# Moving the wait for the output's store from SyncE to GpSimd, which gathers the closing barrier

## The chip, the cores and the metric

One core of a Trainium2 chip. The metric is the device time of one execution in microseconds (us).

The argument plays in the last 2.5 us of a program of 1270 us, so much of it is told in ns. Those numbers are read from the raw records of the traces (start and duration of each instruction, and the time of each semaphore update, to the ns); the views of the profile round starts to 0.1 or 0.01 us. "Landing" is the last increment of the output's semaphore, that is the moment at which the stored output is known to be in memory. "+214" means 214 ns behind the landing of the same trace.

## The reference

Decode attention over a long cache, mixed with a small MLP. Only its shape matters here: 547 MB are read and 1,792 bytes are written.

```python
# K and V cache: [2, 8, 32768, 256] bfloat16 each; x: [2, 1, 448]
def reference(A_x, A_k_cache, A_v_cache, A_wq, A_wo, B_x, B_w1, B_b1, B_w2, B_b2, gate_w):
    x = A_x
    g = _sigmoid((x * gate_w).sum(-1, keepdims=True))
    a = _A_ref(x, A_k_cache, A_v_cache, A_wq, A_wo)      # attention of one query row
    b = _B_ref(x, B_w1, B_b1, B_w2, B_b2)                # gelu MLP
    return g * a + (1 - g) * b                           # [2, 1, 448] bfloat16
```

## The kernel before

Each engine has a program of its own; semaphores order them. GpSimd only prepares constants in the first 5 us. SyncE issues all big loads and, last, the store of the output, for which it waits. The block that holds the five programs ends in a barrier that the language adds: every engine executes a DRAIN, which here ends only after the engine's own last work; the other four then each add one to a gather semaphore, and GpSimd waits for four and releases them.

```python
        def prog_pool(E):
            E.ins(lambda e: e.memset(ident_b[:], 0.0), key="ms0")
            # ... constants, all done after 5.3 us
            for b in range(Bn):
                E.ins(lambda e, b=b: e.affine_select(...), key=f"ts{b}")

        def prog_sp(E):
            # ... every load of weights, K and V
            E.wait_total("mix")                     # both halves of the output are computed
            dma(lambda e: e.dma_start(out[:, 0, :], out_sb), "d_out", "out")
            E.wait_total("d_out")                   # the wait that is moved

        # ... prog_pe, prog_act, prog_dve
        with nc.Block("main") as block:
            def run(nm, eng):
                engs[nm].eng = eng
                progs[nm](engs[nm])

            block.gpsimd(lambda eng: run("pool", eng))
            block.sync(lambda eng: run("sp", eng))
            block.tensor(lambda eng: run("pe", eng))
            block.scalar(lambda eng: run("act", eng))
            block.vector(lambda eng: run("dve", eng))
```

## Time and profile before

| | |
|---|---|
| time, median of 6 runs | 1271.62 us (1271.50 to 1271.81) |
| span of the profiled run | 1269.955 us (shown as 1270.0), its time 1271.76 |
| store issued / landed / last instruction ends | 1268.403 / 1269.558 / 1269.955 us |

The prediction below shows the lines on which the reading rests. One more view helps to calibrate: the program opens with the same barrier as it ends with. These are rows of it (source line 889 of the kernel before: engine, operation, count, then the duration in ns as least/median/most, then the first and last start in us):

```profile
L889 POOLq EVENT_SEMAPHORE  x2: 17/17/17, 0.6 to 0.7; - x2
...
L889 POOLq DRAIN  x1: 187/187/187, 0.3 to 0.3; - x1
...
L889 SPq DRAIN  x1: 121/121/121, 0.5 to 0.5; - x1
```

GpSimd's gather and its release are again 17 ns long and start 79 ns apart (0.607 and 0.686 in the raw records). The recorded duration of such an instruction is a fifth of the step that it costs.

### The profile page before, as it was taken

To read this page: it belongs to the slowest core of one execution; us is meant where nothing else is said; L and a number is where in the kernel's file an instruction comes from. 1 tells how busy PE (TensorE), PEld (TensorE's weight loads), DVE (VectorE), ACT (ScalarE), POOL (GpSimd) and SP (SyncE) were. 2 spreads that over 40 slices of the span, in tenths; PEclk is the share of its full clock that TensorE was granted. 3 is DMA by queue.
4 is the path that set the end of the run, shared out by engine and by line. 5 is a ranking of instruction groups with operands and counts; after the bars stand their busy time and mean duration, and the time that the engine had idled before them with its cause. 6 is when DMAs were issued, how large, how long until landed. Compare 5 with 4: busy or idle time off the path is not lost.

```text
span 1270.0 us, 7459 instructions
## 1 busy us (share of the span) xinstructions
PE 698.5 (55%) x4386; PEld 140.6 (11%) x1842; DVE 689.9 (54%) x311; ACT 44.8 (4%) x184; POOL 4.4 (0%) x19
## 2 busy tenths in 40 slices
PE   0976456644466454565545666444764446655455
PEld 0211011100011110111001111000110001111012
DVE  4575536655365563556735466453665636557351
ACT  0100000000000000000000000000000000000000
POOL 1000000000000000000000000000000000000000
PEclk9877788777788777877768887678877778877787
DMA  9999999999999999999999999999999999999998
GB/s 408 450 429 430 430 431 436 442 431 430 429 431 438 431 438 438 431 431 429 431 438 431 436 440 431 429 431 431 440 429 436 440 431 429 431 431 440 429 425 369
DMA packets 11114, 547.58 MB, mean 431 GB/s; under 512 B 1368, under 2 KB 1632, under 8 KB 2144
## 3 DMA queue, kind: packets, MB, share of 16 engines
q1 hardware_dynamic: 10948, 547.43, 99.7%
q8 instruction: 7, 0.11, 0.0%
q10 hardware_dynamic: 156, 0.01, 0.0%
q14 instruction: 3, 0.02, 0.0%
HBM read 547.43 MB, written 0.00 MB: 431 GB/s over the span
## 4 chain that ended last, share of the span: by engine, by line
DMA 58%; PE 20%; DVE 15%; issue 5%; another core or an unknown queue 2%; ACT 0%; ACTq 0%; SPq 0%; DVEq 0%
DMA ring<-in_A_k_cache_dram 54%; DVE ring L760 12%; PE ps_s L527 7%; PE ps_s L342 6%; PE ps_o L342 4%; DMA ring<-in_A_v_cache_dram 3%; PE ps_o L576 1%; DMA PT<-in_gate_w_dram 1%; DVE mx L764 1%; PE ps_m L541 0%; PE ps_m L536 0%; PE ps_f L588 0%; DVE gmax L766 0%; PE ps_o L470 0%
## 5 line engine op out<-in xcount | busy, mean ns | idle before, releaser
L760 DVE STREAM_TRANSPOSE ring<-ring 128x4096 uint32<-128x4096 uint32 x128 | 557.6, 4413 | 385.0 <-DMA ring<-in_A_k_cache_dram 384.7
L527 PE MATMUL ps_s<-ring,Abd 128*128 128x512 bf16 x1024 | 427.9, 418 | 399.7 <-DVE ring L760 399.2
L342 PE MATMUL ps_s<-ring,Abd 128*128 128x512 bf16 x1024 | 424.4, 414 | 0.0
L527 PEld LDWEIGHTS ps_s<-ring,Abd 128*128 128x128 bf16 x1024 | 106.2, 104 | 822.1 <-DVE ring L760 456.6
L342 PE MATMUL ps_o<-ring,PT 128*24 128x512 bf16 x1504 | 112.0, 405 | 0.0
L546 PE MATMUL ps_f<-o_sb,selg 128*32 128x257 f32 x32 | 17.0, 635 | 91.1 <-DVE o_sb L793 89.9
L576 PE MATMUL ps_o<-ring,PT 128*24 128x512 bf16 x544 | 56.6, 415 | 14.3 <-DMA ring<-in_A_v_cache_dram 14.3
L764 DVE TENSOR_REDUCE mx<-ps_s 128x1 f32<-128x1024 f32 x16 | 19.6, 1225 | 60.8 <-PE ps_s L342 60.8
L677 ACT ACTIVATE negm<-ps_m 128x1 f32<-128x1 f32 x16 | 2.7, 171 | 1133.7 <-PE ps_m L541 1133.7
L777 DVE STREAM_TRANSPOSE PT<-pexp 128x1024 bf16<-128x1024 bf16 x16 | 19.9, 1245 | 36.7 <-PE ps_o L342 36.7
L793 DVE TENSOR_REDUCE o_sb<-ps_o 128x256 f32<-128x2048 f32 x15 | 34.4, 2291 | 0.5
L791 DVE TENSOR_TENSOR ps_o<-ps_o,mask 128x2048 f32<-128x2048 f32 x15 | 34.3, 2290 | 0.0
L576 PEld LDWEIGHTS ps_o<-ring,PT 128*24 128x24 bf16 x544 | 14.5, 98 | 103.9 <-issue 85.2
L774 DVE COPY ls<-lsum 128x1 f32<-128x1 f32 x16 | 2.5, 154 | 32.0 <-ACT pexp L681 32.0
L671 ACT COPY Abd<-qrep 32x16 bf16 (+1 forms) x128 | 19.5, 199 | 0.6
L681 ACT ACTIVATE pexp<-ps_s,negm 128x1024 bf16<-128x1024 f32 x16 | 17.8, 1114 | 1.7
L536 PE MATMUL ps_m<-ident_f,mx 128*1 128x128 f32 x32 | 6.1, 271 | 21.1 <-DVE mx L764 21.1
L441 PE MATMUL ps_o<-ring,xT 128*32 128x512 bf16 x16 | 5.0, 501 | 20.4 <-issue 20.4
L546 PEld LDWEIGHTS ps_f<-o_sb,selg 128*32 128x32 f32 x32 | 2.9, 140 | 109.2 <-DVE o_sb L793 107.1
L541 PE MATMUL ps_m<-ones_f,gmx 1*128 1x1 f32 x32 | 6.3, 262 | 9.9 <-DVE gmx L770 9.9
L807 DVE TENSOR_SCALAR o_sb<-ps_o,mask 128x256 f32<-128x256 f32 x1 | 0.5, 484 | 17.0 <-PE ps_o L342 17.0
L766 DVE TENSOR_REDUCE gmax<-ps_m 1x2 f32<-1x128 f32 x16 | 4.5, 278 | 7.5 <-PE ps_m L536 7.5
(87 smaller groups left out, 75.3 us busy)
## 6 DMA issues: line engine op xcount, KB each, us to landing
ring<-in_A_v_cache_dram SPq DMA_DIRECT2D x1, 4096.0 KB, 27.2
ring<-in_A_v_cache_dram SPq DMA_DIRECT2D x2, 2048.0 KB, 34.0
ring<-in_A_wq_dram SPq DMA_DIRECT2D x1, 3072.0 KB, 28.5
ring<-in_B_w_dram SPq DMA_DIRECT2D x1, 1568.0 KB, 34.5
ring<-in_A_wo_dram SPq DMA_DIRECT2D x1, 1568.0 KB, 37.9
ring<-in_B_w_dram SPq DMA_DIRECT2D x1, 1344.0 KB, 32.2
ring<-in_A_wo_dram SPq DMA_DIRECT2D x1, 1008.0 KB, 39.8
ring<-in_A_wo_dram SPq DMA_DIRECT2D x1, 560.0 KB, 40.7
```

The source lines that it names most:

```text
L342: return e.add_instruction(mybir.InstMatmult(name=f"I-{nc.next_id()}", engine=mybir.EngineType.PE, ldweights=False, ins=[e.lower_ap(x), e. ...
L527: fn = lambda e, o=o, x=x, st=st, sp=sp, s=s, w=w: e.matmul(o, a_win(s, w), x, start=st, stop=sp, skip_group_check=True)
L541: E.ins(lambda e: e.matmul(ps_m[:, C_BC:C_BC + 1], gmx[:, :], ones_f[0:1, 0:1], start=True, stop=True), key=("M2", g))
L546: E.ins(lambda e: e.matmul(ps_oa, selg[:, :], o_sb[:, :], start=False, stop=False, skip_group_check=True), key=("OT", g))
L576: fn = lambda e, o=o, x=x, wt=wt, st=st, sp=sp, j=j: e.matmul(o, wt, x, start=st, stop=sp, skip_group_check=True)
L671: E.ins(lambda e, o=o, Q=Q, c=c: e.copy(o[:, :, c:c + 2], qrep[32 * Q:32 * Q + 32, :, bass.ds(E.dyn(2 * g, 2), 2)]), key=(("A", g) if (Q = ...
L681: E.ins(lambda e: e.activation(pexp[:, :].rearrange("p (r i a) -> p i r a", r=CR, i=2), ps_s[:, :].rearrange("p (i r a) -> p i r a", i=2, ...
L760: E.ins(lambda e: e.transpose(k_words(idx, blk), k_words(idx, blk)), key=("T", idx, blk))
L764: E.ins(lambda e: e.tensor_reduce(mx[:, :], ps_s[:, :], AX.X, ALU.max), key=("MX", g))
L777: E.ins(lambda e: e.transpose(PT[:, :], pexp[:, :]), key=("PT", g))
L791: E.ins(lambda e: e.tensor_tensor(p, p, mb, ALU.mult), key=("OM", g))
L793: E.ins(lambda e: e.tensor_reduce(o_sb[:, 0:Dh], ps_o[:, :].rearrange("p (n d) -> p d n", d=Dh), AX.X, ALU.add), key=("OS", g))
```

## The change

Its intent: GpSimd has to gather the barrier anyway. If it waits for the store itself, SyncE can give its increment early, and the hop from SyncE to GpSimd falls off the end of the program.

```diff
@@ prog_pool
                     fill=1.0, base=256 - 128 * b, pattern=[[-1, 136]], channel_multiplier=-8), key=f"ts{b}")
+            E.wait_total("d_out")
@@ prog_sp
             dma(lambda e: e.dma_start(out[:, 0, :], out_sb), "d_out", "out")
-            E.wait_total("d_out")
-
```

## The prediction

> **What bounds the kernel now.** I read the page first, for the whole span.
>
> ```profile
> span 1270.0 us, 7459 instructions
> ...
> DMA  9999999999999999999999999999999999999998
> ...
> DMA 58%; PE 20%; DVE 15%; issue 5%; another core or an unknown queue 2%; ACT 0%; ACTq 0%; SPq 0%; DVEq 0%
> ```
>
> The 16 DMA engines are 90% busy or more in 39 of 40 slices: the kernel streams its K and V caches (547 MB at 431 GB/s), and that sets the time. The change touches none of it. It concerns what follows the store of the output, so the second view is the timeline of the last microseconds:
>
> ```profile
> 1263.20 4.75 PE L588 MATMUL ps_f<-ring,attnT 128*2 128x224 bf16 x64
> 1268.00 0.34 ACT L697 CAST pexp<-ps_f 2x224 bf16<-2x224 f32 x1 [45.80 <-PE ps_f L588]
> 1268.00 0.38 DVE L846 CAST pexp<-ps_f 2x224 bf16<-2x224 f32 x1 [7.03 <-PE ps_f L588]
> 1268.40 0.33 SPq L413 DMA_DIRECT2D out_dram<-pexp  x1
> ```
>
> The store is issued at 1268.40 and the span ends at 1269.955 (1270.0): 1.55 us. No other change to the time is possible than within these 1.55 us, 0.12% of the span. SyncE's waits say what they are made of; this is the row of its closing wait:
>
> ```profile
> SPq L866 <- DMA out_dram<-pexp: 0.8, 1, 0.8
> ```
>
> SyncE issues for 0.33 us, then stands 0.8 us on the store's landing. Line 866 opens the block that holds the five engines' programs, and its end is put down to that line. The third view is that source line, which shows the closing barrier:
>
> ```profile
> L866 POOLq EVENT_SEMAPHORE  x2: 17/17/17, 1269.8 to 1269.8; - x2
> L866 POOLq DRAIN  x1: 529/529/529, 4.8 to 4.8; - x1
> L866 PEldq DRAIN  x1: 437/437/437, 1267.6 to 1267.6; - x1
> L866 ACTq DRAIN  x1: 368/368/368, 1268.0 to 1268.0; - x1
> L866 DVEq DRAIN  x1: 418/418/418, 1268.0 to 1268.0; - x1
> L866 SPq COMPARE_BRANCH  x1: 33/33/33, 1269.6 to 1269.6; - x1
> L866 SPq DRAIN  x1: 7/7/7, 1269.7 to 1269.7; - x1
> L866 SPq EVENT_SEMAPHORE  x1: 17/17/17, 1269.9 to 1269.9; - x1
> L866 PEldq EVENT_SEMAPHORE  x1: 51/51/51, 1269.9 to 1269.9; - x1
> ```
>
> Four engines drain and add one to a gather semaphore. GpSimd drains too (at 4.8 us: it has been done since then), waits for four (its first EVENT_SEMAPHORE) and releases the others (its second). The wait for the store has no instruction of its own: SyncE's COMPARE_BRANCH, the jump out of its program, carries it. The view rounds starts to 0.1 us; the raw records of the same trace give them to the ns (0 is the span's start). I write the chain with them:
>
> - 1269.558 the store's last increment lands; 1269.574 SyncE's branch starts (+16 ns)
> - 1269.739 SyncE's DRAIN starts (+165 ns after the branch's start, though the branch itself is recorded with 33)
> - 1269.748 its increment of the gather semaphore (+9); 1269.772 GpSimd's gather starts (+24)
> - 1269.850 GpSimd's release starts (+78), 1269.875 its increment is there, 1269.892 to 1269.904 the others pass, 1269.955 TensorE is last to end.
>
> From landing to gather: 16 + 165 + 9 + 24 = 214 ns. From gather to end: 183 ns. TensorE, ScalarE and VectorE gave their increments at 1268.02, 1268.38 and 1268.44, over a microsecond earlier.
>
> **What the Trainium skill says.** "DMA: Bandwidth & Descriptors", section "Why a DMA increments its semaphore by 16 and not by 1": a transfer on k engines has k increments that come with the data, the issuing sequencer writes the other 16 - k at once, and only the full 16 means landed. The trace agrees: the output's semaphore is updated at 1268.845 and then at 1269.526 and 1269.558, for two packets of 896 bytes, so k is 2. Any engine may wait for the 16, and the landing does not move with who waits.
>
> "Perfetto Trace Analysis", section "Sequencer-only Instruction (DRAIN, etc)": the record covers the execution alone; decoding and waiting come before it, and the next instruction is decoded only after the update is pushed. This fits GpSimd's two records of 17 ns that start 78 ns apart, though the second waits for nothing. It matters most below.
>
> "VectorE: DVE Perf Modes", section "The DRAIN you can't avoid": boilerplate DRAINs take some 12 ns. Here it holds only for idle engines: SyncE's 7 ns above. A DRAIN behind running work takes 368 to 529.
>
> "Advanced Engine Details and Errata", section "Control Flow Timing": compare-and-branch some 108 ns. The record here says 33, but the next instruction starts 165 ns after it; I use 165.
>
> **The change part by part.** *Removed:* SyncE's wait. It goes on from its issue (ends 1268.732) to its DRAIN, and its increment should be there by about 1268.9 to 1269.0: I allow the 121 ns that its opening DRAIN took just behind an issue. That is some 0.6 us before the landing, so it is off the path. *Also removed from the path:* the hop from SyncE to GpSimd, 9 + 24 = 33 ns. This is the intent.
>
> *Added:* the same wait on GpSimd, which, by the form that it had on SyncE, will hang on the jump out of GpSimd's program. So GpSimd's own DRAIN, done at 5.3 us before, now comes after the landing, and the gather after the DRAIN. The steps:
>
> - landing to branch on GpSimd: GpSimd's two gathers start 24 ns after the update that frees them (583 to 607 at the opening barrier, 1269.748 to 1269.772 here), SyncE took 16: I take 24
> - branch to DRAIN: 165, as on SyncE (both sequencers show 17 ns for the same EVENT_SEMAPHORE)
> - DRAIN to gather: no wait remains, the four increments are there. One sequencer step of GpSimd without a wait is 78 ns (79 at the opening barrier). I take 78 with an idle DRAIN of about 8
> - sum 267 ns in place of 214.
>
> *Moved:* nothing else. Gather to end stays at 183 ns, as the same instructions follow.
>
> So the change removes a hop of 33 ns and puts a step of 78 and some 8 ns of slower waking there: +53 ns, or +0.004%. 1271.64 + 0.05 = 1271.69 us.
>
> **The rivals.**
>
> *The hop is saved and nothing comes in its place.* If GpSimd's DRAIN overlaps the branch or the gather's decoding, the sum is 24 + 165 + 0 to 30: some 0 to 25 ns faster; and if the jump is cheaper on GpSimd than 165 (VectorE's loop end shows 100 ns from its last branch to the next instruction), up to 90 ns faster. For it: GpSimd's records show that its sequencer runs ahead of its cores (a DRAIN recorded from 4.764 to 5.293 lies over the last AFFINE_SELECT). Against it: the 78 ns step between two instructions that wait for nothing. Time: 1271.55 to 1271.64.
>
> *The DRAIN on GpSimd is long.* Its two records are 187 and 529 ns. For it: there is no record of a short DRAIN on GpSimd. Against it: both contain running work, and end 49 and 66 ns after the last of it (437 to 486, 5.227 to 5.293), as ScalarE's ends 37 ns after its CAST. Even 66 ns of such an answer on an idle engine would only make the +53 into +110; a full 529 would make +0.57. Time: 1271.75, at most 1272.2.
>
> *The wait disturbs something in the stream.* GpSimd's last work ends at 5.2 us and it stood on a semaphore until 1269.77 before as well, so nothing runs later and no buffer comes free at another time. SyncE issues the same transfers in the same order. I see nothing for this rival: 0.
>
> **Range and chances.** Every mechanism moves the time by -0.1 to +0.6 us. The three runs of before already spread over 0.27 us (1271.54 to 1271.81), so which way it goes will hardly show in the times; the range is that spread, widened for another set of runs of a transfer-bound kernel: 1271.2 to 1272.2. Two per cent is 25 us, sixteen times the 1.55 us that the change can reach at all. Same: 0.99; the rest is split for a run that goes wrong for other reasons.
>
> **What would show it right or wrong.** In the trace after: the COMPARE_BRANCH of line 866 is on GpSimd, and none on SyncE; SyncE's DRAIN at about 1268.9; GpSimd's DRAIN after the landing, not at 4.8, with 7 to 70 ns; its gather 240 to 330 ns after the landing in place of 214; its release 78 ns later; the end 183 ns after the gather. A gather less than 214 ns after the landing proves the first rival; a DRAIN over 100 ns the second. A difference in the times beyond 0.6 us, with the landing-to-end stretch as computed, would be scatter of the stream and not the change; one that sits in the tail would make this prediction wrong.

## The result, and the profile after

| | before | after |
|---|---|---|
| time, median of 6 runs | 1271.62 us (1271.50 to 1271.81) | 1271.75 us (1271.68 to 1271.98) |
| ratio | | 1.0001, 95% interval 0.9988 to 1.0014 |

A ratio is the mean time of one kernel's fast runs over that of the other's of the same rounds, so not quite the ratio of the medians quoted. It says "the same". The difference of 0.13 us must not be read as the cost of the change: further down the kernel before, run against itself, differs by 0.16 us. All outputs are right.

The page of the changed kernel shows the same stream:

```profile
span 1269.9 us, 7459 instructions
...
DMA  9999999999999999999999999999999999999998
```

SyncE's own waits in the changed kernel (what it waited for, us in total, times, longest):

```profile
SPq L414 <- DVE pexp L845: 30.9, 1, 30.9
...
SPq L865 <- PEq L865: 1.0, 1, 1.0
```

The wait for the store (0.8 us before) is gone from SyncE; in its place it stands 1.0 us in the barrier. The releaser is inferred: the row names TensorE, but what came at that time was GpSimd's release. SyncE was relieved, and stands just as long.

The closing barrier of the changed kernel (the block's line is now 865):

```profile
L865 POOLq EVENT_SEMAPHORE  x2: 17/17/17, 1269.7 to 1269.8; - x2
...
L865 SPq DRAIN  x1: 142/142/142, 1268.7 to 1268.7; - x1
L865 POOLq COMPARE_BRANCH  x1: 33/33/33, 1269.5 to 1269.5; - x1
L865 POOLq DRAIN  x1: 41/41/41, 1269.6 to 1269.6; - x1
...
L865 PEldq EVENT_SEMAPHORE  x1: 51/51/51, 1269.8 to 1269.8; - x1
```

The COMPARE_BRANCH has gone from SyncE to GpSimd. SyncE's DRAIN is at 1268.7, long before the landing. GpSimd's DRAIN, at 4.8 us before, now stands between the landing and the gather. Against the landing the two chains are, in ns from the raw records:

```text
                            before              after
landing                          0                  0
wait ends (branch starts)      +16 SyncE          +24 GpSimd
DRAIN starts                  +181 SyncE         +173 GpSimd
gather semaphore counts 4     +190               (-606: SyncE's increment, long there)
GpSimd's gather starts        +214               +258
GpSimd's release starts       +292               +336
last instruction ends         +397               +440
```

So the change makes the tail 44 ns longer. That the profiled run of after is nevertheless shorter by 0.06 us (1271.70 to 1271.76) comes from the landing, 1269.460 in place of 1269.558. It is not the stream of K and V: the last load lands at 1267.534 (before: 1267.528). In the trace of before TensorE's last matmuls are 0.1 us further behind that load (the CAST of the result starts at 1267.996, after: 1267.902), and the change does not touch them.

### The profile page after: what moved, and what is told of

Read it like the earlier page. It is cut to its first block, busy times and chain, and to the rows that moved or that the text cites. A ratio compares the mean times of both kernels' runs of the same rounds, so it can differ in the third digit from the quotient of the medians.

```text
span 1269.9 us, 7459 instructions
## 1 busy us (share of the span) xinstructions
PE 699.4 (55%) x4386; PEld 140.4 (11%) x1842; DVE 689.9 (54%) x311; ACT 44.7 (4%) x184; POOL 4.4 (0%) x19
## 4 chain that ended last, share of the span: by engine, by line
DMA 58%; PE 18%; DVE 16%; issue 5%; another core or an unknown queue 2%; ACT 0%; SPq 0%; ACTq 0%; DVEq 0%
DMA ring<-in_A_k_cache_dram 54%; DVE ring L759 14%; PE ps_s L526 6%; PE ps_s L342 5%; PE ps_o L342 4%; DMA ring<-in_A_wo_dram 3%; DVE mx L763 1%; PE ps_o L575 1%; DMA PT<-in_gate_w_dram 1%; PE ps_m L540 0%; PE ps_m L535 0%; DVE gmax L765 0%; PE ps_o L469 0%; DVE gmx L769 0%
## 5 line engine op out<-in xcount | busy, mean ns | idle before, releaser
L342 PE MATMUL ps_o<-ring,PT 128*24 128x512 bf16 x1504 | 115.3, 415 | 0.0
L575 PE MATMUL ps_o<-ring,PT 128*24 128x512 bf16 x544 | 58.4, 428 | 12.6 <-DMA ring<-in_A_v_cache_dram 12.6
```

The source lines that it names most:

```text
L342: return e.add_instruction(mybir.InstMatmult(name=f"I-{nc.next_id()}", engine=mybir.EngineType.PE, ldweights=False, ins=[e.lower_ap(x), e. ...
L575: fn = lambda e, o=o, x=x, wt=wt, st=st, sp=sp, j=j: e.matmul(o, wt, x, start=st, stop=sp, skip_group_check=True)
```

## The experiments

My theory: the tail is a chain of fixed sequencer steps, and the change replaces a hop of 33 ns (9 to SyncE's increment, 24 to GpSimd's gather) by one more step of GpSimd (85 ns) and a wake-up 8 ns slower; the branch step is 16 ns shorter there (149 to 165). 85 - 33 + 8 - 16 = 44. Rivals: the 44 ns are scatter; leaving a program costs the branch step whoever carries the wait; only the recorded duration of GpSimd's DRAIN counts. Each run gives one profile. before_again, after_again, sp_event and late_gpsimd ran on one chip, the next four on a second, late_scalar and pool_drain2 on a third; the times of "before" quoted with a run are of its own chip. The tails can be compared over the chips: both_wait on the second chip repeats the 190 and the 258 of the others. All tails in one place, in ns behind the landing ("last update" is the last of the runtime's closing semaphore, explained at the late_gpsimd run):

| run | landing, us | wait ends | gather | last instruction ends | third / last update | time of this run, us |
|---|---|---|---|---|---|---|
| before | 1269.558 | 16 | 214 | 397 | 876 / 2313 | 1271.76 |
| after | 1269.460 | 24 | 258 | 440 | 914 / 2352 | 1271.70 |
| before_again | 1269.598 | 16 | 214 | 397 | 876 / 2319 | 1271.80 |
| after_again | 1269.681 | 24 | 258 | 441 | 914 / 2357 | 1271.92 |
| sp_event | 1269.797 | 17 | 105 | 289 | 768 / 2208 | 1271.89 |
| late_gpsimd | 1269.730 | 24 | -584 | 41 | 578 / 2020 | 1271.64 |
| late_sync | 1269.477 | 16 | -590 | 33 | 72 / 1509 | 1270.87 |
| after_no_drain | 1269.433 | 24 | 186 | 371 | 851 / 2286 | 1271.61 |
| pool_event | 1269.378 | 24 | 160 | 342 | 816 / 2256 | 1271.52 |
| both_wait | 1269.470 | 17 and 24 | 258 | 440 | 914 / 2351 | 1271.70 |
| late_scalar | 1269.441 | 21 | -594 | 38 | 201 / 1639 | 1270.96 |
| pool_drain2 | 1269.475 | 23 | 169 | 353 | 827 / 2265 | 1271.62 |

In every row landing plus last update is the time of that run plus 0.11 to 0.12 us. So a time is the sum of two parts that can be read apart: when the store lands (it scatters over 0.42 us between these rows) and the tail, which repeats to some ns. From its issue to its landing the store takes 1151 to 1164 ns in all twelve traces, whoever waits for it.

### The two kernels again

No edit. First the kernel before:

> The kernel before, unchanged, against itself: what repeats. My theory (the tail is a chain of fixed steps): landing to gather 214 ns within 15 ns, gather to end 183 ns within 5, although the span moves by 0.1 to 0.3 us. Rival (scatter): landing to gather differs from 214 by tens of ns, so the +44 ns of the change means nothing. Time ratio 1.0000, and its interval shows what the times can resolve.

Measured: landing to gather 214 ns and gather to end 183 ns, exactly as in the first trace. The time: median 1271.83 us (5 runs) against 1271.67 (9 runs) for the same program, ratio 1.0002 (0.9988 to 1.0015). The tail repeats to the ns; the times of identical code differ by more than the change is worth.

> The changed kernel again. My theory: landing to gather 258 ns within 15 ns, so 44 over the kernel before; the median time 0.0 to 0.2 us over that of before, not resolved by the interval. Rival (scatter): 258 does not come back; something between 200 and 270.

Measured: 258 ns again, with the same steps 24, 149, 85. Median 1271.88 us, which is 0.05 over before_again in the same rounds and 0.21 over before, just outside the 0.0 to 0.2 that I gave; ratio to before 1.0001 (0.9988 to 1.0015). Scatter as the cause of the 44 ns falls.

### SyncE waits on an instruction of its own (sp_event)

```diff
             E.wait_total("d_out")
+            E.ins(lambda e: e.nop(nofuse=True))
```

The wait then no longer hangs on the jump out of SyncE's program; the compiled program has a plain semaphore instruction for it, and the jump is gone. (The compiled program has four COMPARE_BRANCH before and three here; after has four, both_wait five, pool_event three. So this jump is compiled only where the wait hangs on it.)

> SyncE waits for the store as before, but an instruction of its own carries the wait in place of the jump out of its program. My theory: the dear part of the old chain was not the hop of 33 ns to GpSimd but the step of 165 ns that the jump takes when it carries the wait; with 16 + a step of 64 to 85 + 33, landing to gather becomes 113 to 134 ns, some 80 to 100 under the kernel before, in the trace; in the time at most 0.1 us, not resolved. Rival (leaving the program costs 165 ns whoever carries the wait): 16 + 64 to 85 + 165 + 33, so 278 to 299 ns.

SyncE's wait has a row of its own in this kernel:

```profile
L415 SPq EVENT_SEMAPHORE  x1: 17/17/17, 1269.8 to 1269.8; - x1
```

and the closing barrier has no COMPARE_BRANCH any more:

```profile
L867 POOLq EVENT_SEMAPHORE  x2: 17/17/17, 1269.9 to 1270.0; - x2
...
L867 SPq DRAIN  x1: 7/7/7, 1269.9 to 1269.9; - x1
```

Measured: from the wait's end at +17 to SyncE's DRAIN at +73 are 56 ns where the jump took 165; the gather starts at +105, so 109 ns sooner than before (expected 80 to 100). Since the compiled program has no jump without the wait, the 109 ns are what the jump costs against a plain instruction; that a wait makes a jump dearer is not shown by this. What was dear in the old chain was the carrier of the wait, not the hop that the change removes: 109 ns against 33. The rival (278 to 299) falls. The time is 1271.73 us (ratio 1.0000, 0.9986 to 1.0013): unresolved, as expected.

### GpSimd waits on an instruction of its own (pool_event)

The same extra instruction behind GpSimd's wait in the changed kernel.

> The changed kernel, but an instruction of its own carries GpSimd's wait in place of the jump out of its program. My theory: the jump that carries the wait costs GpSimd what it cost SyncE, so the branch step of 149 becomes an instruction step of 56 (SyncE's) to 78 (GpSimd's between its two barrier instructions): 24 + 56 to 78 + 85 = 165 to 187 ns from landing to gather, 71 to 93 under the changed kernel and still 60 to 82 over the 105 of the same repair on SyncE. Rival (on GpSimd the step behind the wait is slow whatever carries it): 240 to 260.

```profile
L866 POOLq EVENT_SEMAPHORE  x2: 17/17/17, 1269.5 to 1269.6; - x2
...
L866 POOLq DRAIN  x1: 41/41/41, 1269.5 to 1269.5; - x1
```

Measured in the closing barrier of this kernel: +24, DRAIN at +75 (a step of 51, shorter than I gave it), gather at +160. The jump costs GpSimd nearly as much as SyncE (149 against 51 for a plain instruction, 98 ns more; SyncE 165 against 56, 109 more). The gather came 5 ns sooner than the range that I gave (165 to 187); the rival (240 to 260) falls. And with the dear carrier gone on both engines, waiting on GpSimd is still 55 ns slower than waiting on SyncE (160 to 105). So the placement is the worse one by itself; the jump doesn't explain the loss. The time is 1271.61 us (ratio 0.9999, 0.9984 to 1.0014).

### Without GpSimd's DRAIN (after_no_drain)

```diff
-        with nc.Block("main") as block:
+        with nc.Block("main", no_gpsimd_drain=True) as block:
```

The other four engines still drain; their increments now come from an extra instruction behind the DRAIN, all at least 530 ns before the landing.

> The changed kernel, but GpSimd's DRAIN is left out of the closing barrier (the other four engines still drain). My theory: the step of 85 ns from GpSimd's DRAIN to its gather is what outweighs the saved hop of 33; without it landing to gather is 24 + 149 = 173 ns within 20, under the 214 of before: the change would then be the small gain that it was meant to be. Rival 1 (only the DRAIN's recorded 41 ns count, the rest is the gather's own decoding): 258 - 41 = 217 ns, still no gain. Rival 2 (GpSimd is merely slow to wake): 258 unchanged.

The barrier's rows for GpSimd in this kernel:

```profile
L865 POOLq EVENT_SEMAPHORE  x2: 17/17/17, 1269.6 to 1269.7; - x2
...
L865 POOLq COMPARE_BRANCH  x1: 33/33/33, 1269.5 to 1269.5; - x1
```

Measured: gather at +186, 28 ns under before and 72 under after; expected 173 within 20, so within the range. Neither rival (217, 258) fits. The step removed is thus 72 ns, not 85, because the gather behind the jump needs 162 ns where the DRAIN needed 149. Time 1271.67 us, ratio 0.9999 (0.9984 to 1.0015). With that step gone the change does what it was meant to do; with it, it loses. (The kernel before without GpSimd's DRAIN was not run; that DRAIN is at 4.8 us there, off the path.)

### GpSimd's DRAIN twice (pool_drain2)

```diff
             E.wait_total("d_out")              # in prog_pool
+            E.ins(lambda e: e.drain())         # carries the wait in place of the jump
```

> The changed kernel with GpSimd's DRAIN step doubled: a second DRAIN of its own carries the wait in place of the jump. My theory (each DRAIN on GpSimd is a step of 85 ns even with nothing to drain): landing to gather 24 + 85 + 85 = 194 ns within 10, so 34 over the version where a plain instruction carries the wait (160). Rival (the 85 belong to the first DRAIN behind a wait, or to the gather; a further DRAIN on an empty engine is as short as SyncE's 7 ns and its step the 51 of a plain instruction): 160 ns within 10.

```profile
L372 POOLq DRAIN  x1: 41/41/41, 1269.5 to 1269.5; - x1
...
L866 POOLq DRAIN  x1: 34/34/34, 1269.6 to 1269.6; - x1
```

Measured: the first DRAIN at +23 (41 ns recorded), the second at +91 (34 ns), the gather at +169. My 194 within 10 is wrong, and the rival's 160 within 10 holds. A step of 85 per DRAIN does not exist: it is 68 from DRAIN to DRAIN and 78 from DRAIN to gather, against 51 and 85 with a plain instruction in front (160). Putting a DRAIN in the plain instruction's place adds 9 ns. GpSimd's gather and release, which drain nothing, stand 78 ns apart as well. So the cost looks like that of one more instruction on GpSimd's sequencer, 51 to 85 ns depending on its neighbours, and little of it like the draining. I first held the DRAIN itself guilty; that part of the theory falls. What would show it outright, a plain instruction in the place of the last DRAIN, was not run. The time is 1271.64 us (2 runs; ratio 0.9999, 0.9979 to 1.0019).

### Both wait (both_wait)

SyncE keeps its wait and GpSimd has one too.

> Both SyncE and GpSimd wait for the store, each on the jump out of its program. My theory (the later of two chains sets the gather): SyncE's increment comes at 190 ns, GpSimd stands ready for it only at 258: landing to gather 258 ns within 5, as in the changed kernel. Rival (two engines on one semaphore slow each other, or the chains add): 270 or more.

```profile
L866 SPq COMPARE_BRANCH  x1: 33/33/33, 1269.5 to 1269.5; - x1
L866 POOLq COMPARE_BRANCH  x1: 33/33/33, 1269.5 to 1269.5; - x1
L866 POOLq DRAIN  x1: 41/41/41, 1269.6 to 1269.6; - x1
L866 SPq DRAIN  x1: 7/7/7, 1269.7 to 1269.7; - x1
```

Measured: SyncE's increment is there at +190 and GpSimd's gather starts at +258, as in the changed kernel. Both chains stand in one trace beside the same landing: SyncE's is through 68 ns before GpSimd gets to its gather. This is the plainest proof that the change put the slower chain on the path. The time was 1271.71 us, ratio 1.0000 (0.9985 to 1.0015).

### The wait behind the barrier (late_gpsimd, late_sync, late_scalar)

If the barrier is the cost, no engine need wait for the store before it. One engine waits behind it, as the program's last instruction, so the program still doesn't end before the output has landed.

```diff
             dma(lambda e: e.dma_start(out[:, 0, :], out_sb), "d_out", "out")
-            E.wait_total("d_out")
...
             block.vector(lambda eng: run("dve", eng))
+        nc.gpsimd.wait_ge(sch.streams["d_out"].sem, sch.streams["d_out"].total)   # or nc.sync, nc.scalar
```

> No engine waits for the store before the closing barrier; GpSimd waits for it after the barrier, as its last instruction. The barrier then runs beside the store. My theory: landing to the end of the last instruction 24 + 17 = about 41 ns in place of 397 (before) and 440 (after), so the span ends 0.36 us earlier than before measured from the landing; the time falls by about 0.3 us if what follows the program waits for the last engine only, which the interval may just not resolve. Rival (what follows needs its own 0.2 to 0.3 us behind the four other engines and hides it): landing to end 41 ns but the time unchanged.

Measured: the barrier was over before the landing, and the last instruction ends at +41. Time 1271.40 us against 1271.67, ratio 0.9998 (0.9984 to 1.0011). The tail up to the last update is 299 ns shorter than before (2020 to 2319), not 356: part of the gain was given back behind the program. The rival (time unchanged) falls by the trace; the times alone point the same way but overlap (1271.38 to 1271.64 against 1271.59 to 1272.00).

What lies there? The traces go on with nine updates of semaphore 2, a reset of the kernel's semaphores that begins during the last of them, and nine more updates. The Trainium skill ("Runtime: NRT & Kernel Launch", section "Semaphores 0–2 are reserved") says that number 2 is the runtime's sync barrier. All traces agree with a barrier of the runtime: the device time is 0.11 to 0.12 us less than the stretch from the span's start to its last update. In this run two of the first nine came before the landing, and the third 537 ns behind GpSimd's end. Looking back, in the kernels where GpSimd left the barrier with the others the third came 561 to 568 ns behind GpSimd's last instruction (at +309 before_again, third at +876), each time. That gave the next expectation:

> As with GpSimd waiting behind the barrier, but SyncE waits there. In the traces so far the third update of the runtime's semaphore 2 came 561 to 568 ns behind GpSimd's last instruction when GpSimd left the barrier with the others, and 537 when it waited alone, and the last update followed the third by 1442 to 1443 ns. My theory: GpSimd's own closing is the long one, so with GpSimd free early and SyncE late the last update comes sooner than the 2020 ns behind the landing of the GpSimd version: 1600 to 1900. Landing to the last instruction's end: 16 + 17 = 33 ns. Time 0.1 to 0.4 us under the GpSimd version. Rival (every engine's closing takes as long, so the last to finish sets it): 33 + 537 + 1442 = about 2010, the same as the GpSimd version.

Here GpSimd is through early; these are rows of the barrier of this kernel,

```profile
L865 POOLq EVENT_SEMAPHORE  x2: 17/17/17, 1268.9 to 1269.0; - x2
...
L865 SPq DRAIN  x1: 143/143/143, 1268.7 to 1268.7; - x1
```

and SyncE's wait behind it, with the waits of SyncE:

```profile
SPq L875 <- DMA out_dram<-pexp: 0.5, 1, 0.5
```

Measured: third update at +72, which is 567 behind GpSimd's end at -495; the fifth at +155, 122 behind SyncE's end at +33; the last at +1509, 810 ns sooner than before_again and below the range that I gave (1600 to 1900). Of the 810 ns, 804 are there already at the third update (876 to 72). Time 1270.92 us (1270.80 to 1271.23) against 1271.71 (1271.65 to 1272.00): every run of it is below every run of before, by 0.79 us in the median. The stated ratio is 0.9994 with an interval of 0.9980 to 1.0007, so by that measure alone "same"; the difference in the median (0.79 us) is that of the tails in the traces (0.81 us). It is 0.48 us under the GpSimd version, on another chip; I had given 0.1 to 0.4. The rival (2010) falls.

> As with SyncE waiting behind the barrier, but ScalarE waits there. My theory (the third update of the runtime's semaphore 2 follows GpSimd's last instruction by 537 to 568 ns, and the runtime's chain is otherwise passed from engine to engine): ScalarE's last instruction ends at 21 + 17 = 38 ns; if its update is one of the first two, the third cannot come at 72 as in the SyncE version but waits for ScalarE, by an amount that I do not know (35 to 290 ns behind its end): last update between 1530 and 1960 ns behind the landing, so later than the 1509 of SyncE and earlier than the 2020 of GpSimd. Rival (only GpSimd's closing is long and the position in the chain does not matter): 1509 within 20.

Measured: one update before the landing, the second at +163 (125 behind ScalarE's end at +38), the third at +201, the last at +1639. So ScalarE seems to be second in the runtime's chain, and it holds up everything behind it by some 130 ns; SyncE, which seems to answer fifth, held up nothing that shows (third to last update 1437 ns in late_sync, 1435 to 1443 in all twelve traces). Time 1270.96 us against 1271.82 (ratio 0.9994, 0.9977 to 1.0011). The rival (1509) falls. An engine's answer thus comes 122 to 125 ns behind its end on SyncE and ScalarE, and 537 to 568 on GpSimd. Why GpSimd takes so much longer there is not shown: its closing instructions are not in the traces.

This tells one more thing about the change itself. GpSimd's end moved by 44 ns, but the third update by 38 (876 to 914) and the last by 38 or 39 (2319 to 2357, 2313 to 2352). The cost of the change in device time is 38 ns, 0.003%.

## Why the prediction was right

It said 1271.7 us within 1271.2 to 1272.2; measured 1271.75. The times alone would have let almost any story pass. By its steps:

- *The stream sets the time and is untouched.* Right: 39 of 40 slices at 90% or more before and after, 431 GB/s. The time at which the store lands scatters by 0.42 us over the twelve traces, eleven times the 38 ns of the change.
- *The wait hangs on the jump out of GpSimd's program.* Right: COMPARE_BRANCH on GpSimd, none on SyncE.
- *SyncE off the path.* Right; its increment came at 1268.854. The 1268.9 to 1269.0 given were on the time of before, whose store landed 0.098 us later; on that time it is 1268.952, inside.
- *Waking 24 ns.* Right to the ns, in every GpSimd run but one (23).
- *Branch to DRAIN 165.* 149. A step borrowed from another engine was 16 ns off.
- *DRAIN to gather 78 with an idle DRAIN of about 8.* The step was 85 and the record 41. The idea, one more sequencer step, held, and pool_drain2 speaks for it; the idle DRAIN of 8, borrowed from SyncE, did not.
- *Sum 267 ns in place of 214, so +53.* 258, +44. That it is so near is in part luck: the errors of -16 (branch) and +7 (DRAIN to gather) have opposite signs. Gather to end 183: 182 and 183.
- *Rivals.* "Hop saved, nothing in its place" needed a gather below 214; it is what after_no_drain shows (186), not the change. A DRAIN of over 100 ns did not come. The stream was not disturbed.
- *What it did not see.* It wrote that no change to the time was possible outside the 1.55 us from the store's issue to the span's end. That is wrong, though for this change it did no harm: the device time goes on some 1.8 us behind the span, and who ends late matters there: of late_sync's 810 ns only 364 (397 to 33) lie in the span.

## What to carry to other kernels

Moving a wait to the engine that gathers a barrier saves a hop only if nothing of that engine's own then stands between the event and the gather: list what each engine still has to do behind the awaited event, with steps (start to start), not recorded durations. Look at what carries a wait: here the last jump of a program, compiled only for that, cost 149 to 165 ns, a plain instruction 51 to 56. And the cheapest of the places tried for the wait for the last store was behind the barrier, on an engine that the rest of the closing doesn't hang on (SyncE here, 0.8 us of 1271.7 us; TensorE and VectorE were not tried); differences of this size are read from intervals in the trace, as the times of identical code differ by more.

## What the Trainium skill lacked or had wrong

- "VectorE: DVE Perf Modes", section "The DRAIN you can't avoid": the runtime's boilerplate DRAINs take some 12 ns on all five engines. The DRAINs here are those of the program's own barriers, so the figure is not refuted, but it doesn't carry over to them. An idle SyncE, ScalarE or VectorE shows 7 to 10 ns, but GpSimd, idle for over a millisecond, shows 41 and costs a step of 85 (after, after_again, both_wait, pool_event).
- "Advanced Engine Details and Errata", section "Control Flow Timing": compare-and-branch some 108 ns. The jump that carries the store's wait is recorded with 33 ns and takes 149 (GpSimd) to 165 ns (SyncE) to the next instruction. Where the loops end in the trace of before, branches without a wait took at most 100 (VectorE) and 135 ns (TensorE) to the next instruction, nearer to the page's figure; where the loops go on, 265 to 317. Whether the wait makes the difference is not shown, and no page says it.
- "Runtime: NRT & Kernel Launch", section "The ~15µs preamble/postamble breakdown": gives the closing barrier and resets as whole stages. It lacks which of them a measured device time takes in (here the time follows the last update of semaphore 2), and that they depend on which engine ends last: an answer comes 122 to 125 ns behind the end of SyncE or ScalarE and 537 to 568 behind GpSimd's, so that the same wait cost 2020 ns to the last update on GpSimd, 1639 on ScalarE and 1509 on SyncE.
- No page has the wake-up times: 16 to 17 ns from the last update to SyncE's start, 21 to ScalarE's, 23 to 24 to GpSimd's.
